# Layer 2 of chunk 0 in another order, with the squares of v moved

## The chip, the cores and the metric

The kernel runs on one core of a Trainium2 chip. Times are microseconds (us) of that core for one execution. A core has engines that run side by side, each with its own queue that it works off in order: TensorE (PE, matrix products; PEld is its loading of weights), VectorE (DVE), ScalarE (ACT), GpSimd (POOL) and SyncE (SP). SP and POOL issue most of the transfers between memory and the core. Semaphores make one engine wait for another. Results of PE go into PSUM, from which ACT or DVE has to take them before the place can be written again.

## The reference, cut to what matters

Attention over 8 batches of 8 heads, 576 positions and 64 columns, with a bias from a running sum, and then two dense layers with an exact GELU between them on the 4608 rows that come out:

```python
scores = scale * np.matmul(q, k.transpose(0, 1, 3, 2))
bias = -(cum[:, :, :, None] - cum[:, :, None, :])       # cum = cumsum(max(s, 0))
scores = np.where(causal, -1e9, scores + np.minimum(bias, 0.0))
attn = softmax(scores)                                   # written out in the original
x = (attn @ v).transpose(0, 2, 1, 3).reshape(4608, 512)
h = x @ w_in                                             # 512 -> 2048
out = (0.5 * h * (1 + erf(h / sqrt(2)))) @ w_out         # 2048 -> 512
```

## The kernel before, in words

The rows are worked off in 9 chunks of 512 (`NCH`), the batches of 576 rows one ahead of them: while chunk c goes through the dense layers, batch c+1 goes through attention. The order of the work is written out by hand; each engine gets its instructions in the order in which the Python code issues them, and the framework adds the waits that the data need. A wait is set for whole tiles of PSUM: a matmul into one part of a tile waits until an earlier reader of another part is done.

Layer 1 of a chunk is eight pairs (`l1_item(c, f2)`, L540): each pair fills a tile of two PSUM banks (`h_ps`) with 8 matmuls (L550), and ACT takes it out with a Gelu into `gT` (L558). In chunks 0 and 1 the first two pairs are interleaved, so that the first half of their products, which needs only the first half of `xT`, goes first. Three two-bank slots X, Y, Z are used in turn, in the order that `order[c]` holds; two further banks are M[0] and M[1].

Layer 2 of chunk 0 is four items (`l2_item(c, sub, f0, f1)`, L563), one per 128 rows, of 16 matmuls each (L576) that may be issued in pieces (0 to 8, 8 to 12, 12 to 16). Items 0 and 1 lie in M[0] and M[1], items 2 and 3 are the two halves of one tile in slot Y. After its last piece an item is copied to `o_sb` by ACT or DVE (L402, L404) and stored by SP. The later chunks do layer 2 in another way, by seven products of sums: `sums_b` prepares sums of the weights (`T`, L743), `sums_a` sums of `gT` (`S`, L754), and `prod` multiplies (L764).

Between the pieces of layer 2 of chunk 0 stands the attention of batch 1. `tr_one(1, qd, i, engine, slot)` transposes a tile of q or k on PE (L395) and copies it to `qkT`. `sc_mm(1, p, (z, x))` makes the scores of a pair of heads in two units (L434), in slots Z and X, and ACT takes each out with an exponential into `P` (L440). `mask` multiplies `P` on DVE (L448, L453). `scale_v` multiplies v with the weights of the bias on DVE (L247). `av_main(1, qd, M[qd], slot)` makes one half of the outputs: denominators `av_d` in M[0] or M[1], products `av_o` in a slot (both L463), then four steps on ACT (logarithm L478, exponential L479, twice) and four multiplications into `xT` on DVE (L503). `av_tails` does the last 64 rows in M[0], with two steps on ACT and one multiplication on DVE (L524).

`squares_v(b)` sums the squares of a batch's v on ACT in two instructions (L237), a large one for the first 512 rows and a small one for the last 64; they only feed a test at the end of the kernel. ACT loads a table of functions when it goes from exponentials to Gelus or back (`exp_set`, L863).

The loads of v stand in SP's queue, between the stores of the results; those of q and k in POOL's. `load_qk(3, "k")` of POOL writes into the buffer that v of batch 1 lies in, so it waits for the squares and for `scale_v` of batch 1.

Of the kernel before, what the change touches and what calls it, by code (L numbers as in the profile page):

```python
# [19 lines left out]
def kernel(  # L20
# [10 lines left out]
    nc = tc.nc  # L31
# [11 lines left out]
    ST = 5  # L43
# [3 lines left out]
    SL = S - 512  # L47
# [182 lines left out]
            amx[:, b * NP + p], qkT[b % 2][:, :, p, :S], axis=AX, op=ALU.max, apply_absolute_value=True  # L230
        )

    def squares_v(b):
        t = raws[b, "v"]
        n = work.tile([128, (ST - 1) * H * D], bf16, tag="P", bufs=4, name="junk")
        for j, (n_st, st0, st1) in enumerate(((128, 0, ST - 1), (SL, ST - 1, ST))):
            nc.scalar.activation(  # L237
                n[:n_st, : (st1 - st0) * H * D], t[:n_st, st0:st1].rearrange("p s h d -> p (s h d)"),
                func=AF.Square, accum_out=amv[:n_st, b, j : j + 1],
            )  # L240
# [175 lines left out]
    def tr_one(b, qd, i, eng, slot):  # L416
        t_ps = bank(slot, [128, 2, 16, 64], bf16, "tr_ps")
        tr_mm(b, qd, i, [t_ps[:, pp] for pp in range(2)])
        copy(
            eng, qkT[b % 2][:, i, 2 * qd : 2 * qd + 2, :S].rearrange("d p (t r) -> d p t r", r=FR),  # L420
            t_ps[:, :, :FR].rearrange("d p r t -> d p t r"),
        )
# [115 lines left out]
    order = {0: (X, Y, Z)}  # L538
# [362 lines left out]
    for c in range(NCH):  # L901
        nb = c + 1
        if nb >= B:
            l1_seven(c)
            if c < B:
                order[c + 1] = order[c]
            sums_a(c, (1, 2), HF // 2, HF)
            l2_seven(c)
            continue
        if c < 2:  # L910
            l1_item(c, 0, 0, KO - 2)
            l1_item(c, 1, 0, KO - 2)
            l1_item(c, 0, KO - 2)
            l1_item(c, 1, KO - 2)
        else:
            l1_item(c, 0, 0, KO - 2)
            l1_item(c, 0, KO - 2)
            l1_item(c, 1)
        if 1 < c:
            transpose_tiles(nb)  # L920
            if nb + 1 < B:
                behind_g(qkT[nb % 2][0:1, 1, NP - 1, S - 1 : S])
                for n in "qk":
                    load_qk(nb + 1, n)
        for p in range(NP) if c == 0 else (0, 1) if c == 1 else (0, 1, 2):
            absmax(c, p)
        s0, s1, s2 = order[c]
        for f2 in range(2, FT // 2):
            l1_item(c, f2, slot=(s2, s1, s2, s0, s2, s0)[f2 - 2] if c == 1 else None)
            if c == 1 and f2 in (2, 4):  # L930
                tr_two(2, f2 // 2 - 1, 0, both)
                tr_one(2, f2 // 2 - 1, 1, nc.vector, (s0, s1)[f2 // 2 - 1])
            if c == 1 and f2 == 3:
                squares_v(1)
                load_qk(3, "k")
            if c == 1 and 3 <= f2 < 5:
                scale_v(2, STS[f2 - 3 : f2 - 2], nc.vector)
            if c == 1 and f2 == 5:
                sums_a(c, (1, 2, 3), 0, HF // 2)
                scale_v(2, STS[2:4], nc.vector)  # L940
                squares_v(2)
            if c > 1 and f2 == 3:
                scale_v(nb, [(0, 4), (4, 5)], nc.vector)
                sums_a(c, (1, 2, 3), 0, HF // 2)
                absmax(c, 3)
                if c == B - 2:
                    sums_u((1, 2))
                    absmax(nb, 0)
            if c > 1 and f2 == 4:
                squares_v(nb)  # L950
                if nb + 1 < B:
                    behind(2, raws[nb + 1, "k"][0:1, ST - 2, 0, :])
                    load_v(nb + 1, [nc.sync])
        if c == 0:
            squares_v(0)
            sums_b((1, 2, 3, 4), 0, 4)
            exp_set()
            x, y, z = order[0]
            l2_item(c, 0, 0, 8)
            l2_item(c, 1, 0, 8)  # L960
            tr_one(1, 0, 0, nc.vector, z)
            tr_one(1, 0, 1, nc.scalar, x)
            l2_item(c, 2, 0, 8, y)
            sc_mm(1, 0, (z, x))
            l2_item(c, 3, 0, 8, y)
            sc_mm(1, 1, (z, x))
            mask(1, 0, nc.vector)
            sums_b((1, 2, 3), 4, 8)
            behind(1, w_out_r[0:1, FT - 5, 0:D])
            load_v(1, [nc.sync])  # L970
            l2_item(c, 0, 8, 12)
            l2_item(c, 1, 8, 12)
            tr_one(1, 1, 0, nc.vector, z)
            tr_one(1, 1, 1, nc.scalar, x)
            mask(1, 1, nc.vector)
            sums_b((4,), 4, 8)
            behind_v(1, 1)
            for qd in range(2):
                for n in "qk":
                    load_front(2, n, qd)  # L980
            l2_item(c, 2, 8, 12)
            l2_item(c, 3, 8, 12)
            sc_mm(1, 2, (z, x))
            l2_item(c, 0, 12, eng=nc.scalar)
            sc_mm(1, 3, (z, x))
            mask(1, 2, nc.vector)
            scale_v(1, STS, nc.vector)
            l2_item(c, 1, 12, eng=nc.scalar)
            l2_item(c, 2, 12, eng=nc.scalar)
            mask(1, 3, nc.vector)  # L990
            av_main(1, 0, M[0], z)
            l2_item(c, 3, 12)
            av_main(1, 1, M[1], x)
            av_tails(1, M[0])
            order[1] = (y, z, x)
            load_v(2, [nc.sync])
            load_qk(3, "q")
        else:
            exp_set()
            sums_a(c, (1, 2), HF // 2, HF)  # L1000

            x, y, z = order[c] if c > 1 else (s2, s0, s1)
            order[nb] = (z, x, y)
            add = nc.vector.tensor_tensor
            al_t = bank(M[0], [128, 2, 256], fp32, "o_al")
            al = [al_t[:, u] for u in range(2)]
            kept = [keep_sb(i, n) for i, n in enumerate(("q0", "k0", "q1"))]
            oa = [two_sb() for _ in range(2)]

            prod(c, 1, al, start=True)  # L1010
            sc_mm(nb, 0, (z, x))
            sc_mm(nb, 2, (y,))
            copy(nc.vector, kept[0], al_t)
            if c == 1:
                scale_v(2, STS[4:5], nc.vector)
                load_v(3, [nc.sync])
            be = bank(M[1], [128, 2, 256], fp32, "o_be")
            prod(c, 2, [be[:, u] for u in range(2)], start=True)
            prod(c, 6, al, 0, 6)
            mask(nb, 0, nc.vector)  # L1020
            add(oa[0][:, :, N1], be, kept[0], op=ALU.add)
            sc_mm(nb, 2, (z,), 1)
            sc_mm(nb, 1, (x, y))
            mask(nb, 2, nc.vector)
            prod(c, 6, al, 6)
            copy(nc.vector, kept[1], al_t)
            mask(nb, 1, nc.vector)
            sc_mm(nb, 3, (z, x))
            sums_a(c, (3, 4), HF // 2, HF)
            sums_a(c, (4,), 0, HF // 2)  # L1030
            ga_t = bank(M[1], [128, 2, 256], fp32, "o_ga")
            ga = [ga_t[:, u] for u in range(2)]
            prod(c, 5, ga, start=True)
            mask(nb, 3, nc.vector)
            if nb + 1 < B:
                behind_g(P_of[nb, 3][0:1, 1, PW - 1 : PW])
                cast_qk(nb + 1)
            den = bank(z, [128, 2, 512], fp32, "av_d")
            o = av_pe(nb, 0, den[:, 0], y)
            av_out(nb, 0, den[:, 0], o)  # L1040
            prod(c, 7, al)
            copy(nc.scalar, kept[2], al_t)
            o = av_pe(nb, 1, den[:, 1], x)
            o_t = tails_pe(nb, y)
            add(oa[1][:, :, N2], ga_t, kept[2], op=ALU.add)
            av_out(nb, 1, den[:, 1], o)
            prod(c, 4, al)
            if c == B - 2:
                sums_x(c + 1, nc.vector)
            tails_out(nb, o_t)  # L1050
            copy(nc.scalar, oa[1][:, :, N1], al_t)
            if c == B - 2:
                nc.scalar.preload_act_table_set("gelu_and_others")
            store(c, 2, oa[1])
            prod(c, 3, ga)
            add(oa[0][:, :, N2], ga_t, kept[1], op=ALU.add)
            store(c, 1, oa[0])
            if c == 1:
                absmax(1, 2)
                absmax(1, 3)  # L1060
                square(7)
            elif nb < B - 1:
                square(c + 1 if c > 2 else 0)
            if c == 2:
                cert_decay()
            if c == B - 2:
                sums_u((3,))
# [158 lines left out]
```

## Time and profile before

| | us |
|---|---|
| median of three runs | 311.87 (311.22 to 312.09) |
| profiled execution, as timed | 312.71 |
| its span, first to last instruction | 310.8 |
| PE busy | 291.5 (94%) |
| ACT busy | 247.1 (80%) |
| DVE busy | 227.4 (73%) |
| layer 2 of chunk 0, on PE | 36.10 to 58.70 |
| chunk 1 on PE, both layers | 58.70 to 93.35 |
| a later chunk (chunk 2), on PE | 93.35 to 125.17 |

A row of a timeline has the start, the time from the start of the first to the end of the last instruction of the group, engine, line, operation, the tiles written and read, the number of instructions, and in brackets the idle time before it and what ended it. Matmuls overlap, so the pitch, from one group's start to the next one's, tells more than a group's length. A row of waits has the engine and line that waited, what for, the time in total, how often, and the longest. A row of the chain of waits has start, length and what the work was.

### The profile page before, as it was taken

Reading aid. Unit: us, or ns where it says so; the run is one execution under the profiler, and the core shown is the slowest. Engines: PE = TensorE matmul, PEld = TensorE weight load, DVE = VectorE, ACT = ScalarE, POOL = GpSimd, SP = SyncE. Lnnn points to the kernel's source line nnn. Section 1 sums busy time; section 2 is a strip of 40 time slices with the busy share of each in tenths; the row PEclk is TensorE's granted clock in tenths of the full one; section 3 lists DMA queues with packets and bytes.
Section 4 is the critical chain, followed back from the end, with each engine's and each line's share of the span. In section 5 each row is a group of like instructions: output and inputs, shape, how many; then the busy total and the mean of one; then the engine's idle time right before and its main releaser. Section 6 shows DMA issues by size and latency. Waiting matters only on the chain.

```text
span 310.8 us, 8463 instructions
## 1 busy us (share of the span) xinstructions
PE 291.5 (94%) x3522; PEld 196.3 (63%) x3522; DVE 227.4 (73%) x428; ACT 247.1 (80%) x348; POOL 98.3 (32%) x180
## 2 busy tenths in 40 slices
PE   0789999999999999999999999999999999999990
PEld 0564444555784578457854785478647886887880
DVE  3697347968879787787875697658797888766860
ACT  3786787879977997899788987898879877967830
POOL 6575007105080467137621953095400000000000
PEclk9999999999999999999999999999999999999998
DMA  7999999996707696969597859967990030021022
GB/s 119 195 189 203 207 179 177 278 229 149 148 15 205 120 221 135 251 114 223 116 257 142 193 116 243 199 156 152 210 223 9 2 138 2 0 96 41 2 70 76
DMA packets 77933, 45.07 MB, mean 145 GB/s; under 512 B 63168, under 2 KB 70336, under 8 KB 77888
## 3 DMA queue, kind: packets, MB, share of 16 engines
q1 hardware_dynamic: 67104, 24.93, 34.3%
q0 software_dynamic: 10784, 19.53, 32.3%
q8 instruction: 29, 0.48, 0.7%
q14 instruction: 16, 0.13, 0.1%
HBM read 36.85 MB, written 9.44 MB: 149 GB/s over the span
## 4 chain that ended last, share of the span: by engine, by line
PE 84%; ACT 6%; DVE 4%; DMA 2%; issue 2%; POOL 0%; ACTq 0%; POOLq 0%
PE h_ps L550 31%; PE o_al L764 17%; PE o_ga L764 9%; PE h_ps L667 6%; PE sc_ps L434 5%; PE o_be L764 4%; PE av_o L463 4%; ACT junk L237 3%; PE av_d L463 2%; DMA fk<-in_k_dram 2%; PE o_ps L576 2%; ACT P L440 2%; DVE vv L247 2%; PE tr_ps L395 1%; PE av_t L463 1%
## 5 line engine op out<-in xcount | busy, mean ns | idle before, releaser
L550 PE MATMUL h_ps<-xT,w_in_r 128*128 128x512 f16 x480 | 105.9, 379 | 0.4 <-ACT gT L558 0.3
L550 PEld LDWEIGHTS <-w_in_r 128*128 128x128 f16 x480 | 46.7, 98 | 54.5 <-issue 0.6
L558 ACT ACTIVATE gT<-h_ps 128x1024 f16<-128x1024 f32 x49 | 49.0, 1018 | 18.6 <-PE h_ps L550 18.5
L440 ACT ACTIVATE P<-sc_ps 128x1024 bf16<-128x1024 f32 x64 | 60.2, 1032 | 3.4 <-PE sc_ps L434 3.3
L764 PEld LDWEIGHTS <-S 128*128 128x128 f16 x512 | 48.3, 98 | 8.3 <-issue 0.9
L229 DVE TENSOR_REDUCE amx<-qkT 128x2 f32<-128x1152 bf16 x32 | 41.6, 1344 | 0.6 <-DMA qkT<-qk_bf 0.6
L764 PEld LDWEIGHTS <-gT 128*128 128x128 f16 x384 | 36.4, 98 | 7.0 <-issue 1.3
L448 DVE TENSOR_TENSOR P<-P,tri_bf 128x512 bf16<-128x512 bf16 x64 | 25.9, 419 | 11.3 <-ACT P L440 10.7
L754 DVE TENSOR_TENSOR S<-gT 128x1024 f16<-128x1024 f16 (+1 forms) x30 | 21.6, 721 | 15.1 <-ACT gT L561 13.1
L764 PE MATMUL o_al<-T,S 128*128 128x256 f16 x256 | 31.7, 273 | 0.0
L197 POOL DMA_DIRECT2D raw_k<-in_k_dram x25 | 21.0, 849 | 15.5 <-ACT junk L237 15.5
L434 PE MATMUL sc_ps<-qkT 64*128 64x256 bf16 (+2 forms) x320 | 22.3, 264 | 3.1 <-DVE qkT L404 1.7
L503 DVE TENSOR_TENSOR xT<-av_o,ln 128x256 f16<-128x256 f32 (+2 forms) x72 | 23.7, 385 | 1.7 <-ACT ln L479 1.0
L247 DVE TENSOR_TENSOR vv<-raw_v,wb 128x512 bf16<-128x512 f32 (+2 forms) x25 | 24.0, 1001 | 0.1
L434 PEld LDWEIGHTS <-qkT 64*128 64x128 bf16 x320 | 13.8, 98 | 12.2 <-issue 6.9
L197 POOL DMA_DIRECT2D raw_q<-in_q_dram x25 | 21.1, 857 | 1.2 <-POOL seen_v L148 1.2
L237 ACT ACTIVATE junk<-raw_v 128x2048 bf16<-128x2048 f32 (+1 forms) x16 | 20.3, 1266 | 0.3
L404 DVE COPY qkT<-tr_ps 128x576 bf16<-128x576 bf16 (+1 forms) x13 | 11.7, 938 | 10.4 <-PE tr_ps L395 10.4
L681 DVE TENSOR_TENSOR k<-h_ps,k 128x512 f32<-128x512 f32 (+1 forms) x12 | 11.3, 955 | 8.1 <-PE h_ps L667 5.5
L479 ACT ACTIVATE ln<-ln,lnb 128x256 f32<-128x256 f32 x32 | 16.3, 508 | 1.0
L463 PEld LDWEIGHTS <-vv 128*32 128x32 bf16 x768 | 16.3, 100 | 0.6 <-DVE vv L247 0.2
L463 PE MATMUL av_o<-P,vv 128*32 128x256 bf16 (+1 forms) x512 | 16.7, 272 | 0.0
(132 smaller groups left out, 424.9 us busy)
## 6 DMA issues: line engine op xcount, KB each, us to landing
raw_v<-in_v_dram SPq DMA_DIRECT2D x32, 256.0 KB, 5.1
out_dram<-o_sb SPq DMA_DIRECT2D x14, 512.0 KB, 3.6
raw_q<-in_q_dram POOLq DMA_DIRECT2D x20, 256.0 KB, 4.8
raw_k<-in_k_dram POOLq DMA_DIRECT2D x20, 256.0 KB, 6.9
w_out_r<-in_moe_w_out_dram POOLq DMA_DIRECT2D x4, 512.0 KB, 12.8
out_dram<-o_sb SPq DMA_DIRECT2D x7, 256.0 KB, 6.9
fq<-in_q_dram POOLq DMA_DIRECT2D x6, 288.0 KB, 6.8
fk<-in_k_dram POOLq DMA_DIRECT2D x6, 288.0 KB, 7.8
```

The costliest lines, as they stand in the source:

```text
L197: nc.gpsimd.dma_start(out=t[:n_st, st], in_=src)
L229: nc.vector.tensor_reduce(amx[:, b * NP + p], qkT[b % 2][:, :, p, :S], axis=AX, op=ALU.max, apply_absolute_value=True)
L237: nc.scalar.activation(n[:n_st, : (st1 - st0) * H * D], t[:n_st, st0:st1].rearrange("p s h d -> p (s h d)"), func=AF.Square, accum_out=amv ...
L247: eng.tensor_tensor(vb[:n_st, st0:st1, h0:h1, :], t[:n_st, st0:st1, h0:h1, :], wb[:n_st, st0:st1, b * H + h0 : b * H + h1] .unsqueeze(3).t ...
L434: nc.tensor.matmul(s_ps[:, e, off : off + n], lhsT=qkT[b % 2][e * 64 : e * 64 + 64, 1, p, jt * 128 : jt * 128 + 128], rhs=qkT[b % 2][e * 6 ...
L440: nc.scalar.activation(P[:, :, UO[u] : UO[u] + UW[u]], s_ps[:, :, : UW[u]], func=AF.Exp, scale=scale)
L448: eng.tensor_tensor(d, d, tri_bf.unsqueeze(1).unsqueeze(1).to_broadcast([128, 2, 2, 128]), op=MULT)
L463: nc.tensor.matmul(o[g * 32 : g * 32 + 32, lo : lo + n], lhsT=(wb[:, jt, b * H + 2 * g + qd : b * H + 2 * g + qd + 1].to_broadcast([128, 3 ...
L503: nc.vector.tensor_tensor(xT[:, 2 * qd + t, x0 : x0 + hi - lo], o[t][:, c * 256 + lo : c * 256 + hi], ln[:, c * 256 + lo : c * 256 + hi], ...
L550: nc.tensor.matmul(h_ps[:, i, :], lhsT=w_in_r[:, ko, ft * 128 : (ft + 1) * 128], rhs=xT[:, ko, c * NB % XW : c * NB % XW + NB], start=(ko ...
L558: nc.scalar.activation(gT_of[c][:, f2 * 2 : f2 * 2 + 2, :], h_ps, func=AF.Gelu)
L764: nc.tensor.matmul(o[u], lhsT=lhs[:, f, u * 128 : u * 128 + 128], rhs=rhs[:, f], start=start and j == 0 and (by_sub or u == 0), stop=j == ...
```

## The change

Nothing is computed in another way; instructions stand at other places, and two tasks are cut into smaller ones.

- `squares_v` can do its two instructions apart. In chunk 0 both move from the end of layer 1 into it, behind pair 3. In chunk 1 the large one of batch 1 moves ahead, behind pairs 0 and 1; the small one stays behind pair 3.
- Layer 2 of chunk 0: the first transposes come after item 0 instead of items 0 and 1, and every pair of scores has eight matmuls of layer 2 ahead of it. The outputs of batch 1 (`av_main` twice, `av_tails`) follow each other, with the last pieces of items 0 and 1 ahead and of items 2 and 3 behind them. Item 2 is copied out by DVE and item 3 by ACT; before, it was the other way round.
- `sums_b` of chunk 0 is cut into quarters, the first of them put into layer 1, and the last sum (4 of the second half) is put into layer 1 of chunk 1.
- `scale_v(1)` is cut in two, around a mask.
- The slots of chunk 1 are taken in the order Z, X, Y instead of Y, Z, X.

```diff
-    def squares_v(b):
+    def squares_v(b, js=(0, 1)):
...
-        for j, (n_st, st0, st1) in enumerate(((128, 0, ST - 1), (SL, ST - 1, ST))):
+        for j in js:
+            n_st, st0, st1 = ((128, 0, ST - 1), (SL, ST - 1, ST))[j]
...
             l1_item(c, 1)
+        if c == 1:
+            squares_v(1, (0,))
...
+            if c == 0 and f2 == 3:
+                squares_v(0)
+                sums_b((1, 2, 3, 4), 0, 2)
             if c == 1 and f2 == 3:
-                squares_v(1)
+                squares_v(1, (1,))
                 load_qk(3, "k")
...
                 scale_v(2, STS[2:4], nc.vector)
+                sums_b((4,), 4, 8)
                 squares_v(2)
...
         if c == 0:
-            squares_v(0)
-            sums_b((1, 2, 3, 4), 0, 4)
+            sums_b((1, 2, 3, 4), 2, 4)
             exp_set()
             x, y, z = order[0]
             l2_item(c, 0, 0, 8)
-            l2_item(c, 1, 0, 8)
             tr_one(1, 0, 0, nc.vector, z)
             tr_one(1, 0, 1, nc.scalar, x)
+            l2_item(c, 1, 0, 8)
+            sc_mm(1, 0, (z, x))
             l2_item(c, 2, 0, 8, y)
-            sc_mm(1, 0, (z, x))
+            mask(1, 0, nc.vector)
+            sc_mm(1, 1, (z, x))
             l2_item(c, 3, 0, 8, y)
-            sc_mm(1, 1, (z, x))
-            mask(1, 0, nc.vector)
-            sums_b((1, 2, 3), 4, 8)
+            sums_b((1, 2, 3), 4, 6)
             behind(1, w_out_r[0:1, FT - 5, 0:D])
             load_v(1, [nc.sync])
+            tr_one(1, 1, 0, nc.vector, z)
+            tr_one(1, 1, 1, nc.scalar, x)
             l2_item(c, 0, 8, 12)
             l2_item(c, 1, 8, 12)
-            tr_one(1, 1, 0, nc.vector, z)
-            tr_one(1, 1, 1, nc.scalar, x)
             mask(1, 1, nc.vector)
-            sums_b((4,), 4, 8)
             behind_v(1, 1)
             for qd in range(2):
                 for n in "qk":
                     load_front(2, n, qd)
+            sc_mm(1, 2, (z, x))
+            sums_b((1, 2, 3), 6, 8)
+            scale_v(1, STS[0:2], nc.vector)
             l2_item(c, 2, 8, 12)
             l2_item(c, 3, 8, 12)
-            sc_mm(1, 2, (z, x))
-            l2_item(c, 0, 12, eng=nc.scalar)
+            mask(1, 2, nc.vector)
             sc_mm(1, 3, (z, x))
-            mask(1, 2, nc.vector)
-            scale_v(1, STS, nc.vector)
-            l2_item(c, 1, 12, eng=nc.scalar)
-            l2_item(c, 2, 12, eng=nc.scalar)
+            scale_v(1, STS[2:5], nc.vector)
+            for i in range(2):
+                l2_item(c, i, 12, eng=nc.scalar)
             mask(1, 3, nc.vector)
             av_main(1, 0, M[0], z)
-            l2_item(c, 3, 12)
             av_main(1, 1, M[1], x)
             av_tails(1, M[0])
-            order[1] = (y, z, x)
+            l2_item(c, 2, 12)
+            l2_item(c, 3, 12, eng=nc.scalar)
+            order[1] = (z, x, y)
             load_v(2, [nc.sync])
             load_qk(3, "q")
```

## The prediction

> **What bounds the kernel now.** I read the page first, then who waited for whom on TensorE (PE) in the part that the change touches, the chain of waits, and the timelines of PE, ScalarE (ACT) and VectorE (DVE).
>
> ```profile
> PE 291.5 (94%) x3522; PEld 196.3 (63%) x3522; DVE 227.4 (73%) x428; ACT 247.1 (80%) x348; POOL 98.3 (32%) x180
> ```
> ```profile
> PE sc_ps L434 <- ACT P L440: 0.9, 2, 0.5
> PE h_ps L550 <- ACT gT L558: 0.3, 1, 0.3
> PE sc_ps L434 <- ACT qkT L402: 0.2, 1, 0.2
> ```
> ```profile
> 93.35 13.81 PE h_ps L550 x64
> ```
>
> PE is busy for 94% of the span. From 93.35 us on, the chain of waits is PE alone, chunk after chunk, and the change leaves those chunks as they are. So the change is worth what it does to PE between 36.10 (layer 2 of chunk 0) and 82 us (middle of chunk 1). There PE stood still four times, 1.4 us together by the three wait rows: in chunk 0 before the scores at 42.51 (for the copy of qkT) and in the middle of the last ones behind 51.47, in chunk 1 before the seventh pair of layer 1 (for a Gelu) and before the scores at 80.89 (for an exponential). That is about all that a better order can win.
>
> **The change, part by part.** The durations are in these rows, PE first, then ACT, then DVE:
>
> ```profile
> 36.10 3.62 PE L576 MATMUL o_ps<-w_out_r,gT 128*128 128x512 f16 x16
> 39.65 0.48 PE L395 MATMUL tr_ps<-ident_bf,fq 64*64 64x64 bf16 x36
> ...
> 40.38 1.90 PE L576 MATMUL o_ps<-w_out_r,gT 128*128 128x512 f16 x8
> 42.51 0.61 PE L434 MATMUL sc_ps<-qkT 64*128 64x256 bf16 x10 [0.23 <-ACT qkT L402]
> 43.06 1.90 PE L576 MATMUL o_ps<-w_out_r,gT 128*128 128x512 f16 x8
> 44.89 0.61 PE L434 MATMUL sc_ps<-qkT 64*128 64x256 bf16 x10
> ...
> 47.27 0.48 PE L395 MATMUL tr_ps<-ident_bf,fq 64*64 64x64 bf16 x36
> ...
> 48.12 1.90 PE L576 MATMUL o_ps<-w_out_r,gT 128*128 128x512 f16 x8
> ...
> 51.47 0.39 PE L434 MATMUL sc_ps<-qkT 64*128 64x256 bf16 x4
> ...
> 56.90 0.57 PE L463 MATMUL av_d<-P,wb 128*32 128x256 bf16 x16
> ...
> 58.06 0.29 PE L463 MATMUL av_t<-P,wb 128*32 128x64 bf16 x16
> ...
> 58.70 5.34 PE L550 MATMUL h_ps<-xT,w_in_r 128*128 128x512 f16 x24
> ...
> 64.73 3.63 PE L550 MATMUL h_ps<-xT,w_in_r 128*128 128x512 f16 x16
> ...
> 69.05 1.90 PE L550 MATMUL h_ps<-xT,w_in_r 128*128 128x512 f16 x8
> ...
> 80.89 0.40 PE L434 MATMUL sc_ps<-qkT 64*128 64x256 bf16 x6 [0.42 <-ACT P L440]
> ```
> ```profile
> 34.57 1.02 ACT L558 ACTIVATE gT<-h_ps 128x1024 f16<-128x1024 f32 x1 [0.70 <-PE h_ps L550]
> ...
> 37.27 1.91 ACT L237 ACTIVATE junk<-raw_v 128x2048 bf16<-128x2048 f32 x1
> ...
> 40.05 1.28 ACT L863 ACT_TABLE_LOAD   x1
> ...
> 42.95 1.94 ACT L440 ACTIVATE P<-sc_ps 128x1024 bf16<-128x1024 f32 x2 [0.49 <-PE sc_ps L434]
> ...
> 50.38 1.94 ACT L440 ACTIVATE P<-sc_ps 128x1024 bf16<-128x1024 f32 x2 [1.01 <-PE sc_ps L434]
> 52.21 0.60 ACT L402 COPY o_sb<-o_ps 128x512 f32<-128x512 f32 x1
> ...
> 57.52 0.39 ACT L478 ACTIVATE ln<-av_d 128x256 f32<-128x256 f32 x1 [0.26 <-PE av_d L463]
> ...
> 59.16 0.26 ACT L478 ACTIVATE lnt<-av_t 128x128 f32<-128x128 f32 x1
> 59.45 0.40 ACT L479 ACTIVATE lnt<-lnt,lnb 128x128 f32<-128x128 f32 x1
> ...
> 61.49 1.94 ACT L558 ACTIVATE gT<-h_ps 128x1024 f16<-128x1024 f32 x2 [0.34 <-PE h_ps L550]
> ...
> 72.06 1.90 ACT L237 ACTIVATE junk<-raw_v 128x2048 bf16<-128x2048 f32 x1
> ```
> ```profile
> 57.98 0.68 DVE L404 COPY o_sb<-o_ps 128x512 f32<-128x512 f32 x1
> 58.58 1.47 DVE L503 TENSOR_TENSOR xT<-av_o,ln 128x256 f16<-128x256 f32 x4
> 59.96 0.41 DVE L524 TENSOR_TENSOR xT<-av_t,lnt 128x256 f16<-128x256 f32 x1
> ...
> 76.70 0.69 DVE L754 TENSOR_TENSOR S<-gT 128x1024 f16<-128x1024 f16 x1 [1.46 <-ACT gT L561]
> ```
>
> Pitches, from start to start: eight products of layer 2 take 1.83 (43.06 to 44.89), four that follow others 0.86 (a matmul is 0.216: 13.81 over 64); ten score matmuls 0.55 (42.51 to 43.06); two transposed tiles 0.73 at 39.65 and 0.85 at 47.27; one half of the outputs 1.16 (56.90 to 58.06), the tails 0.64 (to 58.70).
>
> *Squares of chunk 0 into layer 1.* The two squares hold ACT for 2.78 (37.27 to 40.05). Layer 1 leaves ACT 0.70 idle per pair of tiles, and four pairs follow, 2.8 in all. Gelu 3 starts at 34.57 - 3 x 1.73 = 29.4, so the squares end at 33.1 and Gelu 4 at 34.1; pair 7, which wants its bank, starts at 36.10 - 1.73 = 34.4: free, and at most 0.3 of loss if that margin is short. The table load then comes near 37.3 and the copy of qkT is no longer late: the wait before 42.51 goes.
>
> *Layer 2 of chunk 0 up to the last scores.* From 36.10: item 0 to 37.93, transposes 38.66, item 1 40.49, scores 41.04, item 2 42.87, scores 43.42, item 3 45.25, transposes (0.85) 46.10, items 0 and 1 47.93, scores 48.48, items 2 and 3 50.31. Every pair of scores now has eight matmuls ahead of it, as at 44.89, where PE didn't wait; so the wait behind 51.47 goes too. The k tile for the first transposes had landed 12.7 to 12.8 after its issue at 23.8, by 36.6, before the 38.3 at which it is read:
>
> ```profile
> L106 POOL DMA_DIRECT2D fk<-in_k_dram x2: 700/712/725, 23.8 to 26.6; - x2
> ...
> DMA to landing us min/median/max: 12.7/12.8/12.8
> ```
>
> The last scores start at 50.31, before at 51.47: 1.16 gained so far.
>
> *The outputs as one run: a first new wait.* Items 0 and 1 end at 52.69 on PE, but ACT does the exponentials first: they start 0.44 after the scores (42.51, 42.95), at 50.75, and the copy of item 0 follows 1.83 later (50.38, 52.21), from 52.58 to 53.18. The denominators av_d use that bank, M0, so they start at 53.22: 0.5 lost. Its bounds are 0, if ACT copies in time, and 1.0, if item 1's copy came first as well.
>
> *The products behind it: a second new wait, which decides.* Items 2 and 3 share one tile of two banks, and the built program lets the last four matmuls of item 3 wait until item 2 has been copied out (PE waits there for DVE's count at that copy). In the kernel before, ACT did that copy at once. Now DVE does, and in its queue the copy stands behind all nine multiplications of the outputs, which wait for ACT's logarithms and exponentials. From av_d at 53.22: the first logarithm 0.62 later (56.90, 57.52), 53.84; eight steps at 1.64 per four (57.52 to 59.16) to 57.12; the tail's two 0.69 (59.16 to 59.85). On DVE: the eighth step ends near 57.22, two products at 0.35 (58.58 to 59.96 for four) reach 57.96, the tail's product 58.31, the copy (0.68) 58.99. PE starts item 3's last four at 59.04 and layer 1 of chunk 1 at 59.90. Without this wait PE would be ready for them at 53.22 + 2 x 1.16 + 0.64 + 0.86 = 57.04: it stands still for 2.0. Layer 1 starts 1.20 later than at 58.70. The ends of this term: 0.5 less, if the first new wait falls away, and 0.3 more, if each of DVE's last four instructions starts 0.1 late. Behind the waiting matmuls on PE stands all of chunk 1; ACT's copy of item 3, behind them, ends before the Gelus need ACT (2.79 after layer 1's start: 58.70, 61.49).
>
> *Squares of chunk 1 apart.* Before, the squares of v(2) started 13.36 after layer 1 (58.70, 72.06), since those of v(1) held up Gelus 4 and 5. After, v(1)'s large square, about 2.0 with the reading of its sum, lies behind Gelu 1 (a Gelu right behind another starts 0.92 after it: 1.94 for two, less 1.02): it ends 2.79 + 2 x 0.92 + 2.0 = 6.6 after the start, Gelu 2 (1.02) at 7.6, and pair 4 wants its bank at 64.73 + 1.73 - 58.70 = 7.76: just free. Gelu 5 follows its own matmuls at 69.05 + 1.73 + 0.19 - 58.70 = 12.27 (0.19 as from 34.38 to 34.57), the squares of v(2) 0.92 later, at 13.19. That is 0.17 gained. From these squares to the scores at 80.89 ACT works without a pause (Gelus 6 and 7, table load, exponentials), so that stretch only moves; PE still comes early and waits there, and the two waits of chunk 1 bring nothing more. Bounds: 0 (pair 4 late by 0.17) and 0.8 (both waits gone).
>
> *DVE's sums.* Seven instructions more, fourteen of them of half size. One of 1024 elements takes 0.69; I take 0.8 more in all (bounds 0 and 4.8, seven full ones), spread over stretches in which DVE waits. The one moved to chunk 1 fits into the 1.46 before 76.70: nothing; 0.7 if that cover were gone.
>
> *Queues.* SP's loads of v(2) stand behind the stores of items 2 and 3, which come out near 59.0 and 60.7, so they start near 61.1, not 59.10. The last two were issued at 65.5 and 66.3 and landed 4.5 and 3.9 later, by 70.2; the squares want them at 59.90 + 13.19 = 73.1: covered even if all slip by 2.0, with 0.9 to spare. POOL's load of k(3) starts 1 to 2 earlier. The new bank order only renames equal banks.
>
> ```profile
> 59.10 1.37 SPq L225 DMA_DIRECT2D raw_v<-in_v_dram  x2
> ```
> ```profile
> L225 SPq DMA_DIRECT2D raw_v<-in_v_dram x2: 806/1023/1240, 65.5 to 66.3; - x2
> ...
> DMA to landing us min/median/max: 3.9/4.2/4.5
> ```
>
> **Sum.** +1.20 - 0.17 = +1.03 us. The profiled execution took 312.71 (span 310.8 and 1.9 around it) and would take 313.7; the median of the runs, 0.84 lower at 311.87, becomes 312.9.
>
> **Rivals.**
> 1. *No hold.* If item 3 isn't held by item 2's copy, layer 1 starts at 57.04 + 0.86 = 57.9, 0.8 early, and with the 0.17 about 1.0 is gained: 310.9, faster. It decides from a copy that ends before 57.04. Against it speak the built program and the ten steps of ACT that follow 53.84. [...] No row here shows a matmul writing one half of such a tile during a copy of the other.
> 2. *A shorter chain.* If the copy of item 0 comes out in time for av_d, 0.5 of the chain goes and the sum is +0.5: 312.4, no change.
> 3. *Late loads.* If v(2) slips by more than 2.9 (its queue pushed back, k(3) beside it), ACT's chain waits in chunk 1; a slip of 3.5 to 4 costs 0.6 to 1.1 more: 313.5 to 314.0, slower.
>
> **How the numbers follow.** 0.3% (0.94 us) is about what a measurement can tell from no change, so slower begins at 312.81. The forecast's case has 0.58, with 312.3 to 313.3 as its own range: 0.40 of it above that line, 0.18 below. Rival 3 has 0.16 (slower), rival 2 0.18 (same), rival 1 0.08 (faster). Together slower 0.56, same 0.36, faster 0.08. The range goes from 312.1, below rival 2's time, to 313.9, nearly all of rival 3, and leaves out rival 1.
>
> **What would show it.** PE's last four products of item 3 after a gap of about 2 us that DVE's copy of o_ps ends; a gap of 0.5 before av_d that ACT's copy ends; layer 1 of chunk 1 starting near 59.9; no wait before the scores of chunk 0; the squares of v(2) starting 13.2 after layer 1; chunk 2 starting 1.0 later than 93.35. Layer 1 starting before 58.7, or squares that wait for a DMA, would make the forecast wrong.

## The result and the profile after

The changed kernel takes 313.2 us (median of 22 runs, 311.28 to 315.88), the kernel before 312.18 (22 runs beside them, 310.7 to 313.49). The ratio is 1.0045 with a 95% interval of 1.0025 to 1.0066, which is 0.8 to 2.1 us on 312.18 and about 1.4 in the middle. (The ratio goes by means; the medians differ by 1.02.) It is slower, as forecast (312.9, range 312.1 to 313.9).

The profiled execution took 312.61 with a span of 310.8, the same span as before. That is chance: the last matmul starts 1.01 later, and the stretch behind it happened to be shorter. The first row is the kernel before, the second the changed one (timelines of PE).

```profile
301.42 1.91 PE L764 MATMUL o_al<-T,gT 128*128 128x256 f16 x16
```
```profile
302.43 1.91 PE L765 MATMUL o_al<-T,gT 128*128 128x256 f16 x16
```

In the part that the change touches, PE now waits three times. The waits of PE from 20 to 95 us (engine, line, what it waited for: us in total, times, longest):

```profile
PE o_ps L577 <- DVE o_sb L405: 1.9, 1, 1.9
PE av_d L464 <- ACT o_sb L403: 0.5, 1, 0.5
PE sc_ps L435 <- ACT P L441: 0.4, 1, 0.4
```

The two waits in the scores of chunk 0 and the wait for a Gelu in chunk 1 are gone. The first two rows are new, and they are the two that the prediction named. All three come to 2.8 us, where the waits of the same part came to 1.4 before. The time of this part grew by less, 0.91 (below), since other pieces stand closer together: the first half of the outputs takes 1.15 (53.19 to 54.34) where it took 1.40 (54.53 to 55.93). Their places in PE's timeline (start, busy time, form, count, and the idle time before it in brackets):

```profile
36.14 1.89 PE L577 MATMUL o_ps<-w_out_r,gT 128*128 128x512 f16 x8
...
50.23 0.61 PE L435 MATMUL sc_ps<-qkT 64*128 64x256 bf16 x10
...
53.19 0.57 PE L464 MATMUL av_d<-P,wb 128*32 128x256 bf16 x16 [0.52 <-ACT o_sb L403]
...
56.00 1.04 PE L577 MATMUL o_ps<-w_out_r,gT 128*128 128x512 f16 x4
...
58.93 1.02 PE L577 MATMUL o_ps<-w_out_r,gT 128*128 128x512 f16 x4 [1.89 <-DVE o_sb L405]
...
59.79 5.34 PE L551 MATMUL h_ps<-xT,w_in_r 128*128 128x512 f16 x24
...
81.83 0.40 PE L435 MATMUL sc_ps<-qkT 64*128 64x256 bf16 x6 [0.44 <-ACT P L441]
```

At 56.00 item 2's last four run without a pause behind the tails; item 3's last four, which want the other half of the same tile, stand still for 1.89. The reader finds the cause in two queues. First ACT, whose copies of items 0 and 1 stand ahead of the first logarithm, then DVE, where the copy of item 2 stands behind nine multiplications:

```profile
52.55 1.08 ACT L403 COPY o_sb<-o_ps 128x512 f32<-128x512 f32 x2
...
53.80 0.38 ACT L479 ACTIVATE ln<-av_d 128x256 f32<-128x256 f32 x1 [0.17 <-PE av_d L464]
...
57.36 0.40 ACT L480 ACTIVATE lnt<-lnt,lnb 128x128 f32<-128x128 f32 x1
...
59.99 0.59 ACT L403 COPY o_sb<-o_ps 128x512 f32<-128x512 f32 x1 [2.23 <-PE o_ps L577]
...
73.00 1.90 ACT L238 ACTIVATE junk<-raw_v 128x2048 bf16<-128x2048 f32 x1
```
```profile
54.76 3.19 DVE L504 TENSOR_TENSOR xT<-av_o,ln 128x256 f16<-128x256 f32 x8 [1.03 <-ACT ln L480]
57.87 0.41 DVE L525 TENSOR_TENSOR xT<-av_t,lnt 128x256 f16<-128x256 f32 x1
58.20 0.68 DVE L405 COPY o_sb<-o_ps 128x512 f32<-128x512 f32 x1
```

DVE's copy ends at 58.88 and PE goes on at 58.93. From chunk 2 on the chain is PE alone again, as before:

```profile
94.30 13.81 PE h_ps L551 x64
```

The stretch from the start of layer 2 of chunk 0 to chunk 2 is a good ruler, since PE's work in it is the same in all versions, only in another order, and from chunk 2 on they run alike. (The squares of chunk 0 and a part of `sums_b` now lie ahead of it, but layer 1 of chunk 0 takes 13.81 on PE with them, 22.33 to 36.14, and without, 22.29 to 36.10.) It is 93.35 - 36.10 = 57.25 before, 94.30 - 36.14 = 58.16 after, 0.91 more. I call it the stretch below. In four further profiled executions of the changed kernel it came to 58.16 or 58.17. Of the kernel before there is one trace, and in it the second transposes take 0.85 (47.27 to 48.12) where other versions with the same order there take 0.74, so differences from 57.25 are sure only to about 0.1.

### The profile page after: what moved, and what is told of

It is laid out like the page before. It is cut to its first block, busy times and chain, and to the rows that moved or that the text cites. A ratio compares the mean times of both kernels' runs of the same rounds, so it can differ in the third digit from the quotient of the medians.

```text
span 310.8 us, 8466 instructions
## 1 busy us (share of the span) xinstructions
PE 291.1 (94%) x3522; PEld 196.4 (63%) x3522; DVE 228.0 (73%) x435; ACT 247.0 (79%) x348; POOL 98.5 (32%) x180
## 4 chain that ended last, share of the span: by engine, by line
PE 87%; ACT 5%; DVE 3%; DMA 2%; issue 1%; POOL 0%; ACTq 0%; POOLq 0%
PE h_ps L551 32%; PE o_al L765 17%; PE o_ga L765 9%; PE h_ps L668 6%; PE sc_ps L435 5%; PE o_be L765 4%; PE o_ps L577 4%; PE av_o L464 4%; PE av_d L464 3%; DMA fk<-in_k_dram 2%; ACT P L441 2%; PE tr_ps L396 1%; DVE qkT L405 1%; PE av_t L464 1%; ACT junk L238 1%
## 5 line engine op out<-in xcount | busy, mean ns | idle before, releaser
L577 PE MATMUL o_ps<-w_out_r,gT 128*128 128x512 f16 x64 | 15.4, 380 | 1.9 <-DVE o_sb L405 1.9
```

What stands on the lines that cost most here:

```text
L577: nc.tensor.matmul(o_ps, lhsT=gT[:, ft, sub * 128 : (sub + 1) * 128], rhs=w_out_r[:, ft], start=(ft == 0), stop=(ft == FT - 1),)
```

## The experiments

Theory A is the prediction's account: the whole loss is the hold of item 3's last four matmuls by the copy of item 2, less small gains elsewhere. Theory D, which some of the later expectations name, is that a long stop of PE also lowers PE's clock for a while behind it. Each edit is shown against the changed kernel unless it says otherwise.

**Both matmul groups ahead of the copies.** `l2_item` is split, so that the copy and the store stand in a function of their own, `l2_out`.

```diff
-            l2_item(c, 2, 12)
-            l2_item(c, 3, 12, eng=nc.scalar)
+            l2_item(c, 2, 12, out=False)
+            l2_item(c, 3, 12, out=False)
+            l2_out(c, 2)
+            l2_out(c, 3, nc.scalar)
```

> The changed kernel with one edit: the last four matmuls of items 2 and 3 both stand ahead of the two copies, so item 3 no longer waits for the copy of item 2. Theory A (the hold costs what the trace shows, and nothing takes its place): the 1.9 us gap on PE goes, layer 1 of chunk 1 starts near 57.8 instead of 59.8, the 0.5 gap before av_d stays, and the kernel is 2.0 us faster than the changed kernel and 0.9 to 1.0 us (0.3%) faster than the kernel before. Rival B (ACT's chain in chunk 1 takes it back, because the squares of v(2) then wait for their loads, which landed at 70.8 in the changed kernel): the squares start at 70.8 or later instead of 71.0, and 0.5 us or more of the gain is gone. Rival C (the loss sits elsewhere): within 0.3 us of the changed kernel.

Measured: 310.75 (12 runs) against 311.87 (35 runs of the kernel before beside them, as in the next experiments), ratio 0.9958 [0.9943, 0.9972], faster than before. The stretch is 92.64 - 36.46 = 56.18: 1.98 less than the changed kernel, 1.07 less than before. Waits and timeline of PE, and the chain:

```profile
PE av_d L464 <- ACT o_sb L403: 0.5, 1, 0.5
PE sc_ps L435 <- ACT P L441: 0.4, 1, 0.4
```
```profile
56.32 1.90 PE L577 MATMUL o_ps<-w_out_r,gT 128*128 128x512 f16 x8
58.06 5.13 PE L551 MATMUL h_ps<-xT,w_in_r 128*128 128x512 f16 x23
```
```profile
92.64 13.81 PE h_ps L551 x64
```

The eight matmuls are one group now, and the row with 1.9 us is gone. So the hold is made by the order in which the program asks for the copy and the matmuls, and it is worth 2.0 us. All else that the change does is a gain of about 1.1.

**Item 2's matmuls ahead of the products too.** This asks whether the 0.5 before av_d can go as well.

```diff
             mask(1, 3, nc.vector)
+            l2_item(c, 2, 12, out=False)
             av_main(1, 0, M[0], z)
...
-            l2_item(c, 2, 12)
-            l2_item(c, 3, 12, eng=nc.scalar)
+            l2_item(c, 3, 12, out=False)
+            l2_out(c, 2)
+            l2_out(c, 3, nc.scalar)
```

> As copies_behind, and the last four matmuls of item 2 stand ahead of the outputs, where PE waited 0.5 us for ACT's copy of item 0. Theory A: that gap goes too, layer 1 of chunk 1 starts near 57.3, and the kernel is 1.4 to 1.5 us (0.45%) faster than the kernel before. Rival B (ACT's chain and the loads of v(2) set the end of that stretch): layer 1 starts as early, but the squares of v(2) wait for a load until about 70.8 and the kernel is no faster than copies_behind, 0.7 to 1.0 us faster than before.

Measured: 311.28 (12 runs), ratio 0.9966 [0.9952, 0.9979]. The stretch is 56.51, 0.74 less than before, but 0.33 more than with the copies behind alone. The wait before av_d is gone and a new one stands in layer 1 of chunk 1. Waits of PE, then ACT and PE:

```profile
PE h_ps L551 <- ACT gT L559: 0.5, 1, 0.5
PE sc_ps L435 <- ACT P L441: 0.4, 1, 0.4
```
```profile
60.16 0.59 ACT L403 COPY o_sb<-o_ps 128x512 f32<-128x512 f32 x1 [1.15 <-DVE o_sb L405]
60.77 1.28 ACT L559 ACT_TABLE_LOAD   x1
62.06 1.94 ACT L559 ACTIVATE gT<-h_ps 128x1024 f16<-128x1024 f32 x2
```
```profile
58.13 5.62 PE L551 MATMUL h_ps<-xT,w_in_r 128*128 128x512 f16 x24
```

Neither theory named this. ACT's copy of item 3 waits 1.15 for DVE's copy of item 2 (the two share the tile in PSUM and the tile `o_sb` that they write; which of them sets this wait was not tested), and the table load for Gelu stands behind it. The first Gelu starts at 62.06, 3.93 after layer 1 (58.13), where 2.79 was enough before. What PE no longer waits for at av_d, it waits for at a Gelu. The other 0.3 lie in the first 24 matmuls of layer 1, which take 5.62 here and 5.34 in the changed kernel. I put it down to `xT`: the last exponential that the eighth multiplication into it needs ends here at 58.42 (57.91 + 0.51), 0.29 behind the start of layer 1; in the changed kernel it ended at 57.17 (56.66 + 0.51), 2.62 ahead of it. No row shows that wait itself.

**The same, with the table load ahead of the copies.**

```diff
             l2_item(c, 3, 12, out=False)
+            nc.scalar.preload_act_table_set("gelu_and_others")
             l2_out(c, 2)
             l2_out(c, 3, nc.scalar)
```

> As item2_ahead, and ScalarE loads the Gelu table ahead of the copy of item 3, for which it waits until VectorE has copied item 2 (in item2_ahead the table load began only at 60.77 and the first Gelu at 62.06, 3.9 us after the start of layer 1). Theory A: the first Gelu starts 2.8 us after layer 1, chunk 2 1.0 us earlier than in item2_ahead, and the kernel is 0.5 to 0.6% faster than the kernel before. Rival B: the squares of v(2) then wait for their loads (landed near 70.8) and half of this is lost.

Measured: 310.66 (6 runs) against 312.15 (23 runs), ratio 0.9937 [0.9912, 0.9962], the lowest of all, though the intervals of the two versions above reach into its own. The stretch is 55.90, 1.35 less than before and the shortest of all. ACT, then the only wait of PE that is left in the list:

```profile
58.65 1.28 ACT L1005 ACT_TABLE_LOAD   x1
59.95 0.58 ACT L403 COPY o_sb<-o_ps 128x512 f32<-128x512 f32 x1
60.82 1.94 ACT L559 ACTIVATE gT<-h_ps 128x1024 f16<-128x1024 f32 x2 [0.29 <-PE h_ps L551]
```
```profile
PE sc_ps L435 <- ACT P L441: 0.4, 1, 0.4
```

The load lies in the time in which ACT waited anyway; the Gelu now waits for PE and not PE for it. This version beats both kernels.

**Only the squares of chunk 0** (against the kernel before). Layer 2, products and outputs stay in their old order.

```diff
+            if c == 0 and f2 == 3:
+                squares_v(0)
...
         if c == 0:
-            squares_v(0)
```

> The kernel before with one edit: the squares of chunk 0 stand in layer 1, behind pair 3. Theory A: the 0.23 us wait of PE ahead of the first scores goes, and layer 1 of chunk 0 isn't held up; layer 1 of chunk 1 starts 0.2 to 0.3 us earlier, unless the copies behind take it; 0.0 to 0.3 us (under 0.1%) faster. Rival (pair 7 waits for Gelu 4): layer 1 of chunk 0 ends up to 0.3 us later and nothing is won.

Measured: 311.79 (12 runs), ratio 0.9997 [0.9981, 1.0013], no difference in the times. In the trace the stretch is 56.82, 0.43 less. Waits of PE:

```profile
PE sc_ps L434 <- ACT P L440: 0.9, 2, 0.5
PE h_ps L550 <- ACT gT L558: 0.3, 1, 0.3
```

The wait for the copy of qkT is gone, as forecast. The 0.43 is more than the 0.2 to 0.3 that was expected; about 0.1 of it is the transposes of the one trace before. 0.43 us is 0.14%, which the times can't tell from nothing.

**Only the squares of chunk 1** (against the kernel before).

```diff
-    def squares_v(b):
+    def squares_v(b, js=(0, 1)):
...
+        if c == 1:
+            squares_v(1, (0,))
...
-                squares_v(1)
+                squares_v(1, (1,))
```

> The kernel before with one edit: the large square of batch 1 stands behind pairs 0 and 1 of chunk 1, the small one stays. Theory A (ACT works without a pause from the squares of v(2) to the scores, so only their earlier start counts): the 0.34 us wait of PE for a Gelu goes, the wait ahead of the scores at 80.9 grows instead, and chunk 2 starts 0.17 us earlier. Rival (both waits of chunk 1 were due to the place of the squares): both go, and chunk 2 starts 0.7 to 0.8 us earlier.

Measured: 312.21 (12 runs), ratio 1.001 [0.9995, 1.0025], no difference. The trace has 56.99, 0.26 less. Waits of PE:

```profile
PE sc_ps L435 <- ACT P L441: 1.0, 2, 0.5
...
PE sc_ps L435 <- ACT qkT L403: 0.2, 1, 0.2
```

The wait for a Gelu is gone. Of the 0.26, 0.11 lies in layer 2 of chunk 0, which this edit doesn't touch (the transposes again); chunk 1 itself is 0.15 shorter (58.62 to 93.12, before 58.70 to 93.35), where 0.17 was forecast. The scores of chunk 1 still wait 0.43, as Theory A had it: ACT works without a pause from the squares of v(2) to there, so only their shift counts.

**The engines of the two copies exchanged.** ACT copies item 2, DVE item 3.

```diff
-            l2_item(c, 2, 12)
-            l2_item(c, 3, 12, eng=nc.scalar)
+            l2_item(c, 2, 12, eng=nc.scalar)
+            l2_item(c, 3, 12)
```

> The changed kernel with the engines of the two copies swapped: ScalarE copies item 2 behind its ten steps, VectorE item 3. Theory A: ScalarE is free near 57.8, the copy ends near 58.3, layer 1 of chunk 1 starts near 59.2 instead of 59.8 and chunk 2 0.55 us earlier than in the changed kernel; PE stands still 1.3 us there. Theory D: with the shorter gap fewer than 9 in 22 executions have the mean clock of 0.987 to 0.989. Rival: if the place of the copy, and not the chain ahead of it, set the time, nothing changes.

Measured: 312.2 (12 runs) against 312.15, ratio 0.9995 [0.9976, 1.0013]. The stretch is 57.50, 0.66 less than the changed kernel (0.55 forecast).

```profile
59.09 1.02 PE L577 MATMUL o_ps<-w_out_r,gT 128*128 128x512 f16 x4 [1.25 <-ACT o_sb L403]
```

The hold follows the engine that copies: ACT's queue comes to the copy 0.64 earlier than DVE's. In the same comparison the changed kernel stands at 313.46, so the times differ by 1.26, more than the 0.66 of the trace. That is a first sign of a second cost, no more: the intervals of the two ratios reach 0.6 and 0.8 us to either side.

**The changed kernel again**, unchanged, beside these.

> The changed kernel once more. Theory D: 3 to 7 of 12 executions have the mean clock of 0.987 to 0.989 and take about 1.9 us more than the others; where the profiled one is among them, its trace shows some 3 to 4 us at half clock right behind the gap between 57 and 59. Rival (that clock is a state of the chip that the first measurement met by chance): none, or as few as among the executions of the kernel before beside it.

Measured: 313.46 (12 runs), ratio 1.0048 [1.0022, 1.0074]. The result holds. But the 34 executions of both series, the 22 of the result and these 12, fall apart by PE's mean granted clock (1 is full speed all the time). Twenty have 0.994 or more; 14 have 0.986 to 0.989. In the first series those took 314.63 on the mean, the others 312.71; here 314.68 and 313.20. No execution of the kernel with copies behind (0 of 12) or with exchanged copies (0 of 12) has a clock in that group, and of the kernel before 1 of 67 has one (0.987, at 313.02 us). The other low clock in these runs, 0.981 to 0.984, comes with the kernel before too (5 of 23 here) and costs little there (312.55 against 312.19); in the one trace that has it (the version with the table load ahead), the low clock lies early: 0.58 on the mean of 15 to 23 us, 1.00 ahead of it and from 23 to 60. In the trace of the kernel before it is 1.00 from 15 to 23. The columns are the window, its length, the busy time of PE, PEld, DVE, ACT and POOL with their counts, the granted clock, the DMA share and GB/s:

```profile
15.00:23.00 8.00, 6.06 (x153) 5.23 (x151) 7.06 (x19) 6.59 (x13) 7.08 (x14) 0.58 1.11 171
```

**A longer hold.** DVE gets two more reductions, of 1.3 us each, ahead of the copy of item 2. They are moved there from layer 1 of chunk 1.

```diff
-        for p in range(NP) if c == 0 else (0, 1) if c == 1 else (0, 1, 2):
+        for p in range(NP) if c == 0 else () if c == 1 else (0, 1, 2):
...
+            for p in range(2):
+                absmax(1, p)
             l2_item(c, 2, 12)
```

> The changed kernel with the two maxima of chunk 1 (2.6 us of VectorE) put ahead of the copy of item 2, so that PE stands still for 4.5 us there instead of 1.9. Theory A (only the wait counts): 2.6 us slower than the changed kernel in its time and in the start of chunk 2, with the granted clock of the executions spread as for the kernel before. Theory D (a stretch in which PE stands still long enough also lowers its clock for a few us afterwards; in 9 of 22 executions of the changed kernel the mean clock was 0.987 to 0.989 and the time 314.6 on average, against 312.7 in the other 13; no execution of the first four experiments had that clock together with such a time): most executions have a mean clock near 0.987 or lower and take 4 us or more longer than the changed kernel's 312.7, and the trace shows a stretch of half clock behind the gap.

Measured: 318.83 (6 runs) against 312.15, ratio 1.0185 [1.015, 1.022]; all six took 316.56 or more. The stretch is 63.42, 5.26 more than the changed kernel, of which the gap explains only 2.5 (4.4 for 1.9). Wait, and windows with the columns above:

```profile
PE o_ps L577 <- DVE o_sb L405: 4.4, 1, 4.4
```
```profile
62.00:65.00 3.00, 2.13 (x6) 0.73 (x6) 0.82 (x2) 0.23 (x1) 0.00 (x0) 0.50 0.50 181
65.00:68.00 3.00, 3.00 (x9) 1.04 (x8) 0.00 (x0) 1.64 (x2) 0.00 (x0) 0.50 0.56 149
68.00:71.00 3.00, 3.00 (x14) 1.31 (x13) 0.00 (x0) 1.74 (x2) 0.00 (x0) 0.93 1.31 239
```

PE comes back from the gap at half clock: nine matmuls in 3 us where the last window has fourteen. The remaining 2.7 us are this.

**Three single executions of the changed kernel, each with its trace**, to catch the low clock in one.

> The changed kernel, one profiled execution, to meet one with the mean clock of 0.986 to 0.989 (14 of 34 so far). Theory D: in such an execution the granted clock is 0.5 for 3 to 4 us from within or right behind the gap between 57 and 59, and chunk 2 starts 1.7 to 2.0 us later than the 94.30 of the trace shown. Rival: the half clock lies at the start or the end of the execution, where the clocks of 0.98 of the kernel before may lie, which cost little.

> The changed kernel, a second profiled execution. Theory D: if its mean clock is 0.986 to 0.989, 3 to 4 us at half clock right behind the gap between 57 and 59, and chunk 2 1.7 to 2.0 us later than in the trace shown. Rival: half clock at the start or the end instead.

> The changed kernel, a third profiled execution. Theory D: if its mean clock is 0.986 to 0.989, 3 to 4 us at half clock right behind the gap between 57 and 59, and chunk 2 1.7 to 2.0 us later than in the trace shown. Rival: half clock at the start or the end instead.

Measured: 313.34, 313.7 and 312.12 us with clocks of 0.995 and 0.996. None has the low clock (that makes 14 of 37 in all), so they settle nothing about where it falls. All show the stretch at 58.16 or 58.17 and so confirm the cost of the wait itself.

**A hold in between.** One reduction ahead of the copy instead of two.

```diff
-        for p in range(NP) if c == 0 else (0, 1) if c == 1 else (0, 1, 2):
+        for p in range(NP) if c == 0 else (1,) if c == 1 else (0, 1, 2):
...
+            absmax(1, 0)
             l2_item(c, 2, 12)
```

> As hold_long with one of the two maxima ahead of the copy of item 2: PE stands still for about 3.1 us there, between 1.9 (changed kernel, 14 of 34 executions with the lower clock) and 4.4 (hold_long, 6 of 6). Theory A: 1.25 us slower than the changed kernel's executions at a clock of 0.99 or more, so 314.1 to 314.5 in all executions. Theory D: more than 14 in 34 but perhaps not all of the executions have a mean clock of 0.989 or less and take 1.7 us more, 315.8 to 317; where the profiled one is among them, its granted clock is 0.5 for 3 to 7 us behind the gap. Rival: the drop needs a gap of more than 3.1 us, and the share stays as it was.

Measured: 317.0 (5 runs, 316.44 to 317.39) against 312.35 (9 runs), ratio 1.015 [1.0128, 1.0173]. The stretch is 62.34, 4.18 more than the changed kernel: 1.26 from the gap (3.15 for 1.89) and 2.9 from the clock. Wait and timeline of PE, then windows:

```profile
PE o_ps L577 <- DVE o_sb L405: 3.1, 1, 3.1
```
```profile
60.28 1.87 PE L577 MATMUL o_ps<-w_out_r,gT 128*128 128x512 f16 x4 [3.15 <-DVE o_sb L405]
```
```profile
57.00:61.00 4.00, 0.85 (x3) 0.26 (x2) 3.94 (x7) 0.82 (x3) 0.00 (x0) 0.80 1.05 324
61.00:64.00 3.00, 3.00 (x8) 1.06 (x7) 0.49 (x1) 1.80 (x2) 0.00 (x0) 0.50 0.84 260
64.00:67.00 3.00, 3.00 (x10) 1.17 (x9) 0.00 (x0) 0.22 (x2) 0.00 (x0) 0.63 1.03 241
67.00:70.00 3.00, 3.00 (x84) 1.55 (x81) 0.13 (x1) 3.00 (x3) 0.00 (x0) 1.00 1.10 203
```

The same window in the changed kernel's profiled execution, right behind its gap, has the full clock and fifteen matmuls:

```profile
60.00:63.00 3.00, 3.00 (x15) 1.37 (x14) 1.40 (x2) 2.28 (x3) 0.00 (x0) 1.00 1.04 324
```

The four held matmuls take 1.87 instead of 1.02. All five times lie within 1 us, so every execution paid about the same; Theory D had given 315.8 to 317 for a part of them. But their mean clocks go from 0.976 to 0.992, with 317.0 us at 0.992: the mean clock alone doesn't tell for sure whether an execution paid.

## Why the prediction was right

The sign and the cause were right, and nearly every step came out as the prediction put it:

- *Layer 2 of chunk 0 up to the last scores:* forecast at 50.31, measured 50.23, with no wait in chunk 0's scores; the second transposes took 0.74 instead of the 0.85 read from the trace before. The gain up to here is real: with the hold taken away, the changed order is 1.07 faster than before in the trace and 0.4% in the times.
- *Squares of chunk 0 into layer 1:* no loss, and the wait for qkT goes. Done alone it brought 0.43 in the trace.
- *First new wait:* 0.5 forecast, 0.52 measured, by the copy of item 0, with av_d at 53.19 instead of 53.22.
- *Second new wait:* 2.0 forecast, 1.89 measured; layer 1 of chunk 1 starts 59.79 - 36.14 = 23.65 after layer 2, where it was 58.70 - 36.10 = 22.60: 1.05 later (1.20 forecast). This term was 0.15 too large, over DVE's last instructions, which ended 0.11 earlier than forecast.
- *Squares of chunk 1:* those of v(2) start 73.00 - 59.79 = 13.21 after layer 1, before 13.36: 0.15 gained (0.17 forecast). The scores of chunk 1 still wait, 0.44.
- *Queues:* the last load of v(2) was issued at 66.9 and landed 3.9 later, at 70.8; in the kernel before it was 70.2. The squares want it at 73.0, so the cover held.
- *Sum:* +1.03 forecast, +0.91 measured in the stretch.

Of the rivals, *No hold* (310.9) was the one whose condition mattered. It did not come true, but its price was right: the kernel with both matmul groups ahead of the copies takes 310.75. In that kernel, too, no matmul writes item 3's half while item 2's is copied; the matmuls come first. What the runs show is only that the built program orders the tile as a whole (1.89 us of wait); what the chip would do without that order was not shown. *A shorter chain* (312.4) did not come true; when the chain was shortened from the other side, by ACT's copy of item 2, the kernel took 312.2. *Late loads* are not to be seen: the squares at 73.00 wait for nothing.

One thing was missing from the sum: PE's clock behind the gap. The wait explains 0.91, and 0.91 lies within the interval of 0.8 to 2.1, so the times alone don't ask for more. What asks for more is how the executions fall apart: in the first series, 13 at full clock take 312.71 on the mean and 9 at 0.987 to 0.989 take 314.63, 1.9 more. Shared out over the series, that adds 9/22 x 1.9 = 0.8, and 0.91 + 0.8 = 1.7 lies within the interval too. So it is partly luck that the medians differ by 1.02, almost as forecast (1.03): the 13 executions alone lie 0.6 above the mean of the kernel before (312.09), and the nine others draw the middle up.

That the low clock follows a gap in this place is shown for 3.1 and 4.4 us. For the 1.9 us of the changed kernel it is only inferred, from the group's absence where the gap is 1.25 or nothing (but for one execution of the kernel before): none of the changed kernel's five profiled executions had it, so where the clock drops in those that do stays open. What makes 14 executions differ from the other 20 is open too.

## What to carry to other kernels

When two accumulations share a tile of two banks, issue all their matmuls before the first copy, since in a program that sets its waits by whole tiles the copy of one half holds the matmuls into the other: here for 1.89 us, and the stretch was 1.98 shorter without it. Before a copy is given to another engine, read that engine's queue ahead of it: here nine multiplications cost PE 1.9 us, while the same order without the hold gains 1.1. Price a long gap of PE above its length: here one of 3.15 us cost 2.9 more and one of 4.41 cost 2.7 more, and with one of 1.9 us 14 of 34 executions had a lower clock and took 1.5 and 1.9 us longer than the others on the mean of their series. And look behind each wait that goes for the next one: here it was a table load (1.28 us), which could be drawn ahead into time in which ACT waited anyway.

## What was not expected of the hardware

Two gaps of PE cost twice here. With the gap of 3.15 us (57.13 to 60.28) the granted clock was 1.00 from 36 to 57, 0.80 on the mean of 57 to 61, 0.50 from 61 to 64, 0.63 from 64 to 67 and 1.00 from 67 on. If it was either full or half, these means put it at half from about 59.4 to 66.2, well into the next layer: from 2.3 us after PE stopped, for 6.8 us. With the gap of 4.41 us (58.46 to 62.87) it was 1.00 from 36 to 58, 0.95 from 58 to 62, 0.50 from 62 to 68, 0.93 from 68 to 71 and 1.00 from 71 on, which in the same way is half from about 61.6 to 68.4: from 3.1 after PE stopped, for 6.8 again. The price was 2.9 and 2.7 us on top of the gaps. In both traces PE worked without a pause from the end of the gap on, and the clock was still at half for about 5.9 and 5.5 us.

Behind a shorter gap the traces show no such fall. With the 1.89 and 1.90 us of the changed kernel's profiled execution and of its repetition the clock was 1.00 from 57 to 69 and from 57 to 95; in the three single executions, with 1.9 us of wait each, the stretch is as long as there (58.16 or 58.17). With the 1.25 us of the exchanged copies it was 1.00 from 57 to 95. So the traces have the fall at 3.15 and 4.41 us and not at 1.9. What makes the clock fall, why it took 2.3 us in one gap and 3.1 in the other, and what ends the half clock was not shown, and of the 14 executions with the low clock there is no trace. Counted over the executions, the cost came with the longer waits: 6 of 6 by their times at 4.4 us, 5 of 5 at 3.1, 14 of 34 by their mean clock at 1.9, none of 12 at 1.25.
